# Two layers of attention and routed SwiGLU on one core: gathering early candidates for the eight routed tokens while the last token tile is projected

## The chip, the cores and the metric

The kernel runs on one core of one Trainium2 chip, and the seven other cores are idle. The metric is the device time of one execution in microseconds. The time shown for the kernel before is the median of three runs, 4652.86 us (4651.84 to 4653.18).

The engines named below are PE (TensorE, matrix products, with PEld for its weight loads), DVE (VectorE), ACT (ScalarE), POOL (GpSimd) and SP (SyncE, which only issues transfers). A transfer is issued on the queue of SP, ACT or POOL. Each engine works through its own instructions in the order in which the program lists them.

## The reference

The sequence has 2048 tokens of width 1024, all in float32. Four blocks follow one another, with x carried along: attention, routed feed-forward, attention, routed feed-forward, the same weights both times. "Layer 0" and "layer 1" below are the two pairs.

```python
def A(x, wqkv, wo):                  # 32 heads of 32
    q, k, v = split(x @ wqkv)
    return softmax(q @ k.T * 32 ** -0.5) @ v @ wo        # per head
def B(x, w_r, w_gate, w_up, w_down): # F = 3584
    r = x @ w_r                      # one score per token
    idx = argsort(-r)[:8]            # the eight best of 2048 tokens
    x_sel = x[idx]
    y = (silu(x_sel @ w_gate) * (x_sel @ w_up)) @ w_down
    return x + scatter(y * sigmoid(r[idx]), idx)         # other rows: x
x = A_x
x = x + A(layernorm(x)); x = x + B(layernorm(x))
x = x + A(layernorm(x)); x = x + B(layernorm(x))
```

What is computed for the eight tokens needs all of w_gate, w_up and w_down: 44 MB, read once per layer.

## The kernel before, in words

Each layer has three stages: projection of q, k and v; attention over 32 units of 16 key tiles; and the output projection, a loop over 16 token tiles `t` of 128 rows. The output loop (lines 922 to 960) multiplies a tile by `wo` in three passes, each of 16 matmuls of 512 columns: `woh` with the high part of the attention output, `woh` with the low part, `wol` with the high part. Then DVE adds the residual (L934), takes mean and variance (L130, L132), POOL takes the power -0.5 (L134, L135), DVE normalises into `xn` (L951) and reduces `xn` times `w_r` into one column of `rcols` (L952): the router scores of the tile. POOL writes mean and factor of each row to `mr` (L943 to L946), which goes to the DRAM tensor `mrd` (L949), adds `x + xn` (L953), and the sum is stored to the layer's output (L956). SP issues both stores, except in tile 15 of layer 1, where ACT does.

After the loop `route` runs. `top8` finds the eight best scores: PE transposes `rcols` (L280), DVE takes the best eight of each tile (L283), spreads them over one row by a product with `own` (L284, L286), takes the best eight of that row and their places (L289, L290), and turns places into token numbers by small products (L293 to L312). Two gathers by POOL (L197) then read the eight rows of the output, `bg`, and their mean and factor, `mg`, from DRAM. DVE rebuilds the normalised rows (L347), PE transposes them in eight pieces (L350), and DVE copies the result into `xs` (L351), the stationary operand of the feed-forward.

In layer 0 `exchange` runs between: the eight routed rows change places with the last eight rows of the sequence, so that layer 1 can start on tiles 0 to 14 before the feed-forward of layer 0 is done. It gathers rows into `tg` and scatters them (L197, L201). Layer 1 begins by loading tiles 0 to 2 of its input (`xt`, SP, L74), normalising them (L130 to L563) and transposing them on PE (L572), after five steps of layer 0's feed-forward and four more; the rest of that feed-forward is spread between the matmuls of the q, k, v projection. In layer 1 `back` undoes the exchange with two gathers and two scatters, and the feed-forward follows by itself, up to the end of the kernel.

The feed-forward is a list of steps, each with one weight tile of 1 MB at most: `g` and `u` (gate and up, eight each, for columns 0 to 2047 and then for the rest, rows of 8 KB and 6 KB), `t` (transposes) and `d` (down: for each half of 512 output columns seven tiles of 512 rows by 512 columns, 2 KB a row), `y` (the sum over four row groups by a product with `sel`, L413, the gate factor and the residual, L415). Each step multiplies on PE (L376, L403); down steps add up in SBUF on DVE (L409). Weight tiles are loaded by SP (L184 for down, L188 for gate and up). In layer 1 22 tile slots exist: ten of their own, loaded during the output loop, and twelve that stand on the tiles of the output loop as these come free (`ord` after tile 13; `woh`, `wol`, `ohl` after tile 15). Another load can start only when a step has used up its tile.

Of the kernel before, what the change touches and what calls it, by code (L numbers as in the profile page):

```python
# [19 lines left out]
NT = S // 128  # L20
# [37 lines left out]
def tile_kernel(ctx, tc, x, wqkv, wo, w_r, w_gate, w_up, w_down, out):  # L58
# [42 lines left out]
    sel = cons.tile([128, 8], F32, name="sel")  # L101
    dve.tensor_add(sel, ident[:, 0:8], ident[:, 32:40])
    dve.tensor_add(sel, sel, ident[:, 64:72])
    dve.tensor_add(sel, sel, ident[:, 96:104])

    triu = cons.tile([128, 128], F32, name="triu")
# [5 lines left out]
    ones_c = cons.tile([8, 128], F32, name="ones_c")  # L112
    pool.memset(ones_c, 1.0)
# [4 lines left out]
    pool.iota(first_of, pattern=[[1, 1]], base=0, channel_multiplier=128, allow_small_or_imprecise_dtypes=True)  # L118
    ones16 = cons.tile([NT, 128], F32, name="ones16")
    pool.memset(ones16, 1.0)  # L120
    PERM = {}
# [16 lines left out]
    class FeedForward:  # L138
# [6 lines left out]
        def __init__(self, n, dst, mrd):  # L145
# [7 lines left out]
            for b in range(2):  # L153
                self.steps += [("d", b, c) for c in range(7)] + [("y", b, 0)]
# [20 lines left out]
        def load(self, eng=sync):  # L175
# [7 lines left out]
            if k == "d":  # L183
                eng.dma_start(t.rearrange("p (i m) -> p i m", i=4),  # L184
                              w_down[a * 512:(a + 1) * 512, h * 512:(h + 1) * 512].rearrange("(i p) m -> p i m", p=128))
            else:
                w = (w_gate if k == "g" else w_up)[a * 128:(a + 1) * 128, h * 2048:min((h + 1) * 2048, F)]
                eng.dma_start(t[:, 0:w.shape[1]], w)  # L188

        def more(self, wp, names):  # L190

            self.pools += [(wp, i, k) for i, k in names for _ in range(k)]
            for _ in range(sum(k for _, k in names)):
# [13 lines left out]
        def exchange(self, sb, idx):  # L207
# [6 lines left out]
            dve.tensor_scalar(ne, sb[:, 2:10], tcol, None, op0=OP.not_equal)  # L214
# [5 lines left out]
            pe.matmul(p[0:8, 0:1], triu[0:8, 0:8], ni, start=True, stop=True)  # L220
            pe.matmul(p[0:8, 8:16], ltb, triu[0:8, 0:8], start=True, stop=True)
# [15 lines left out]
            tg = self.tmp.tile([8, D], F32, name="tg")  # L237
# [33 lines left out]
        def top8(self, rcols):  # L271
# [3 lines left out]
            t = self.tmp.tile([128, D], F32, name="x", bufs=3) if n else self.tmp.tile([NT, 512], F32, name="t8")  # L275
            r16, vals, toks = (t[0:NT, 128 * i:128 * i + 128] for i in range(3))
            row = t[0:1, 384:512]
            rows8 = lambda a: a.rearrange("p (a b) -> p a b", b=8)
# [716 lines left out]
```

## Time and profile before

| | |
|---|---|
| median of three runs | 4652.86 us |
| profiled execution | 4661.98 us |
| its span, first to last instruction | 4660.2 us |
| output loop and `route` of layer 0: last product of tile 15 to first matmul of layer 1's projection | 2246.2 to 2280.2 us |
| the same of layer 1: last product of tile 15 to first product of the feed-forward | 4552.7 to 4581.5 us |
| feed-forward of layer 1, to its last scatter | 4581.5 to 4652.9 us |

Times in the profile count from the start of the span. A row of a timeline gives start, duration, engine, line, operation, what it writes and reads, shapes, the number of instructions merged, and in brackets the idle time of the engine before and what ended it. PEq, SPq and so on mark the issuing part of an engine. A row of the windows view gives the length of the stretch, the busy time and instructions of each engine (PE, PEld, DVE, ACT, POOL), then the granted TensorE clock as a share of full speed, the share of the 16 DMA engines that was busy, and the GB/s they moved.

### The profile page before, as it was taken

Reading aid. Unit: us, or ns where it says so; the run is one execution under the profiler, and the core shown is the slowest. Engines: PE = TensorE matmul, PEld = TensorE weight load, DVE = VectorE, ACT = ScalarE, POOL = GpSimd, SP = SyncE. Lnnn points to the kernel's source line nnn. Section 1 sums busy time; section 2 is a strip of 40 time slices with the busy share of each in tenths; the row PEclk is TensorE's granted clock in tenths of the full one; section 3 lists DMA queues with packets and bytes.
Section 4 is the critical chain, followed back from the end, with each engine's and each line's share of the span. In section 5 each row is a group of like instructions: output and inputs, shape, how many; then the busy total and the mean of one; then the engine's idle time right before and its main releaser. Section 6 shows DMA issues by size and latency. Waiting matters only on the chain. (4 is left out here: it accounts for less than half of the span.)

```text
span 4660.2 us, 76410 instructions
## 1 busy us (share of the span) xinstructions
PE 4536.3 (97%) x30704; PEld 2758.9 (59%) x30704; DVE 3169.7 (68%) x4855; ACT 2430.3 (52%) x2564; POOL 3214.3 (69%) x1240
## 2 busy tenths in 40 slices
PE   8999999999999999989899999999999999999995
PEld 8888755555555555548677887555555555554581
DVE  2211588888888888866422215888888888887762
ACT  2222266766767676750122222776766767677400
POOL 4444378988989888944433342898889889898441
PEclk9999999999999999999899999999999999999997
DMA  5766476776867777759689674777777768676698
GB/s 184 207 183 192 137 168 147 172 158 151 180 147 169 161 168 156 176 119 263 196 255 277 199 206 128 163 169 155 169 150 168 164 146 182 149 168 160 149 252 307
DMA packets 350899, 833.40 MB, mean 179 GB/s; under 512 B 43760, under 2 KB 192240, under 8 KB 301376
## 3 DMA queue, kind: packets, MB, share of 16 engines
q1 hardware_dynamic: 297216, 477.44, 35.7%
q0 software_dynamic: 44960, 325.34, 34.3%
q10 hardware_dynamic: 8368, 25.73, 2.1%
q8 instruction: 241, 3.95, 0.4%
q14 instruction: 114, 0.93, 0.1%
HBM read 384.07 MB, written 119.24 MB: 108 GB/s over the span
## 5 line engine op out<-in xcount | busy, mean ns | idle before, releaser
L503 DVE TENSOR_REDUCE nm<-st 128x1 f32<-128x512 f32 x3896 | 2419.0, 683 | 402.2 <-PE st L495 396.1
L819 ACT ACTIVATE P<-pre 128x1024 f32<-128x1024 f32 x2048 | 1986.2, 1022 | 716.1 <-PE pre L510 517.8
L755 POOL TENSOR_TENSOR acc<-acc,P 128x2048 f32<-128x2048 f32 x434 | 2104.0, 4848 | 80.0 <-DMA P<-P 71.8
L510 PE MATMUL pre<-q,ks 64*128 64x512 f32 (+1 forms) x8192 | 1141.6, 396 | 4.2 <-ACT P L819 4.2
L745 PE MATMUL pv<-P,v 128*32 128x512 f32 x8192 | 1091.0, 605 | 2.6 <-DMA v<-vd 2.6
L495 PEld LDWEIGHTS st<-ks,q 64*128 64x128 f32 x3896 | 542.6, 184 | 905.2 <-DVE nm L503 764.7
L495 PE MATMUL st<-ks,q 64*128 64x512 f32 x3896 | 975.8, 470 | 0.5
L549 POOL TENSOR_TENSOR wl<-wraw,wh 128x2048 fp32r<-128x2048 f32 (+1 forms) x101 | 443.3, 4391 | 657.0 <-ACT wh L548 616.7
L510 PEld LDWEIGHTS pre<-q,ks 64*128 64x128 f32 (+1 forms) x8192 | 774.2, 186 | 185.5 <-ACT P L819 57.2
L758 POOL DMA_DIRECT2D P<-P x310 | 297.1, 958 | 261.4 <-PE st L495 192.0
L604 DVE TENSOR_TENSOR lo<-st,hi 128x512 fp32r<-128x512 f32 x128 | 88.3, 690 | 526.6 <-ACT hi L603 517.4
L589 PE MATMUL st<-xh,wh 128*128 128x512 f32 x1024 | 408.3, 399 | 0.0
L589 PE MATMUL st<-xh,wl 128*128 128x512 f32 x1024 | 399.7, 390 | 4.2 <-POOL wl L549 4.2
L589 PE MATMUL st<-xl,wh 128*128 128x512 f32 x1024 | 399.6, 390 | 0.0
L603 ACT CAST hi<-st 128x512 fp32r<-128x512 f32 x128 | 75.3, 588 | 550.4 <-PE st L589 546.2
L745 PEld LDWEIGHTS pv<-P,v 128*32 128x32 f32 x8192 | 161.8, 108 | 259.1 <-issue 253.5
L755 POOL TENSOR_TENSOR acc<-P 128x2048 f32<-128x2048 f32 x62 | 294.6, 4751 | 8.4 <-DVE nm L503 4.5
L589 PE MATMUL st<-wh,xh 128*128 128x256 f32 x1024 | 294.2, 287 | 2.3 <-ACT wh L548 2.0
L589 PE MATMUL st<-wl,xh 128*128 128x256 f32 x1024 | 291.2, 284 | 2.1 <-POOL wl L549 2.1
L589 PE MATMUL st<-wh,xl 128*128 128x256 f32 x1024 | 290.9, 284 | 0.8 <-DVE xl L575 0.8
L929 PE MATMUL pre<-woh,ohl 128*128 128x512 f32 x1024 | 245.3, 397 | 20.0 <-DVE pre L952 13.0
L589 PEld LDWEIGHTS st<-xh,wh 128*128 128x128 f32 x1024 | 192.4, 188 | 74.5 <-issue 27.9
(228 smaller groups left out, 3186.8 us busy)
## 6 DMA issues: line engine op xcount, KB each, us to landing
P<-P POOLq DMA_DIRECT2D x310, 1024.0 KB, 8.9
wraw<-in_A_wqkv_dram SPq DMA_DIRECT2D x96, 1024.0 KB
q<-qh SPq DMA_DIRECT2D x256, 128.0 KB
ks<-kh SPq DMA_DIRECT2D x112, 256.0 KB
vd<-vn SPq DMA_DIRECT2D x64, 256.0 KB
qh<-hi SPq DMA_DIRECT2D x64, 256.0 KB
ql<-lo SPq DMA_DIRECT2D x64, 256.0 KB
kh<-hi SPq DMA_DIRECT2D x64, 256.0 KB
```

Of the source, the lines that this page charges most:

```text
L495: pe.matmul(ps[b], Q[u][rows, i, 0, qt * 128:(qt + 1) * 128], KS[(u // QC) % 2][rows, i, 0, j * 512:(j + 1) * 512], start=True, stop=True, ...
L503: dve.tensor_reduce(NM[u][:, j, 2 * i + b:2 * i + b + 1, qt], ps[b], axis=AX.X, op=OP.max, negate=True)
L510: pe.matmul(p[:, b * 512:(b + 1) * 512], KS[(u // QC) % 2][rows, i, slot, kt * 128:(kt + 1) * 128], Q[u][rows, i, slot, :], start=(slot == ...
L549: pool.tensor_tensor(wl[:, sl, :], raw[:, sl, :], wh[:, sl, :].bitcast(F32), op=OP.subtract)
L589: pe.matmul(p, *pair(a, l, r), start=(a == 0 and k == 0), stop=(a == KD - 1 and k == 2))
L603: act.copy(hi, p)
L604: dve.tensor_tensor(lo, p, hi.bitcast(F32), op=OP.subtract)
L745: pe.matmul(PV[u][32 * h:32 * h + 32, :], V[g][:, kt, 32 * h:32 * h + 32], P[s][:, h, :], start=(kt == 0), stop=(kt == NT - 1), tile_posit ...
L755: (dve if on_dve else pool).tensor_tensor(o, a, P[u * NT + k].rearrange("p h c -> p (h c)"), op=OP.add)
L758: pool.dma_start(P[u * NT + a], P[u * NT + b], accum_op=OP.add)
L819: act.activation(P[s][:, 2 * i:2 * i + 2, :].rearrange("p h c -> p (h c)"), p, AF.Exp, scale=SCALE)
L929: pe.matmul(p[:, bl], l[:, a, :], r[a][:, bl], start=(k == 0 and a == 0), stop=(k == 2 and a == KD - 1))
```

## The change

Five edits go together, in both layers unless said.

1. `top8` is gone. `candidates` finds the best eight of tiles 0 to 14 in three parts while tile 15 is projected: the first part stands in front of the third matmul pair of the third pass, the second in front of the seventh pair, the third between the normalisation and the score reduction of tile 15. It ends with gathers of the eight candidates' output rows and of their mean and factor.
2. `route` takes the best eight of these eight and of the 128 scores of tile 15. The rows of `xs` come by one-hot matrix products: for each of eight pieces of 128 columns one product of `xn` (tile 15, still in SBUF) with a 128 x 8 selection and one of the candidates' rows with an 8 x 8 selection, in place of eight transposes. In layer 1 the token numbers, the gather of `bg`, `back` and `token` come after `xs`; in layer 0 they and `exchange` come before.
3. Down weights come as full rows: 14 tiles of 256 rows by 1024 columns, 4 KB a row, with the two column halves side by side in the row groups of PSUM, so one list of 14 `d` steps and one `y` step with two products by `sel` and two DVE operations.
4. In layer 1 one `ohl` slot is loaded after tile 14, and tile 14's two stores go from SP to ACT. Tile 15 writes no `mr` and no `mrd` row in either layer.
5. Layer 0 closes the loop's tiles after `route`, and `route` has its scratch in them; `sel` has two columns of eight and a few constants are new.

```diff
+        def candidates(self, rcols, wp):
+            tiny, m = self.tiny, NT - 1
+            t = wp.tile([128, D], F32, name="x", bufs=3)
...
+            pe.transpose(p[0:m, 0:128], rcols[:, 0:m], ident)
+            dve.tensor_copy(r, p[0:m, 0:128])
...
+            dve.max(m16, r)
+            dve.tensor_tensor(rows8(vals), own[0:m, 0:m, :], m16[:, None, :].to_broadcast([m, m, 8]), op=OP.mult)
+            yield
+            p = ps_st()
+            pe.matmul(p[0:1, 0:8 * m], ones16[0:m, 0:1], vals, start=True, stop=True)
...
+            dve.max_index(mi, final[:, 0:8], row)
...
+            dve.tensor_tensor(rows8(toks), own[0:m, 0:m, :], f16[:, None, :].to_broadcast([m, m, 8]), op=OP.mult)
+            yield
+            p, c = ps_st(), slice(0, 8 * m)
+            pe.matmul(p[:, 0:8], ones_c[0:1, :], mif, start=True, stop=True)
+            pe.matmul(p[c, 16:24], toks, ones16[0:m, 0:8], start=True, stop=True)
+            pe.matmul(p[c, 24:25], vals, ones16[0:m, 0:1], start=True, stop=True)
...
+            self.rows = wp.tile([128, D], F32, name="x", bufs=3)[0:8]
+            self.mg = tiny([8, 2], "mg")
+            self.gather(self.rows, idx, self.dst[0:S - 128, :])
+            self.gather(self.mg, idx, self.mrd[0:S - 128, :])
...
+            pe.transpose(p[0:1, 0:128], rcols[:, NT - 1:NT], ident)
+            dve.tensor_copy(final[:, 8:136], p[0:1, 0:128])
...
+            if not n:
+                sb, PERM["routed"] = tokens()
+                self.exchange(sb, idx=PERM["routed"])
+            dve.tensor_scalar(self.rows, self.rows, self.mg[:, 0:1], self.mg[:, 1:2], op0=OP.subtract, op1=OP.mult)
...
+                pe.matmul(p[:, a, 0:8], xn[:, sl], pl, start=True, stop=False)
+                pe.matmul(p[:, a, 0:8], self.rows[:, sl], pc, start=False, stop=True)
+            dve.tensor_copy(xs[:, :, 0:8], p[:, :, 0:8])
...
-                eng.dma_start(t.rearrange("p (i m) -> p i m", i=4),
-                              w_down[a * 512:(a + 1) * 512, h * 512:(h + 1) * 512].rearrange("(i p) m -> p i m", p=128))
+                eng.dma_start(t.rearrange("p (i m) -> p i m", i=2),
+                              w_down[a * 256:(a + 1) * 256, :].rearrange("(i p) m -> p i m", p=128))
...
+                part = ffn.candidates(rcols, wp) if t == NT - 1 else None
                 for k, (l, r) in enumerate(((oh, woh), (ol, woh), (oh, wol))):
                     for a in range(KD):
+                        if part and k == 2 and a in (2, 6):
+                            next(part)
...
+                if n and t == NT - 2:
+                    ffn.more(wp, (("ohl", 1, 2),))
...
+                store = act if n and t >= NT - 2 else sync
+                if t < NT - 1:
...
                 dve.tensor_scalar(xn, x2, mv[:, 0:1], rs, op0=OP.subtract, op1=OP.mult)
+                if part:
+                    list(part)
                 dve.scalar_tensor_tensor(p, xn, 1.0, wrb, op0=OP.mult, op1=OP.mult, accum_out=rcols[:, t:t + 1])
```

More of the change, by code (lines that the diff above doesn't have):

```diff
@@ L190, in more @@
         def more(self, wp, names):
[L192 to L193 removed]
+            self.pools += [(wp, i, bufs) for i, k, bufs in names for _ in range(k)]
+            for _ in range(sum(k for _, k, _ in names)):
                 self.load()
```

205 lines of the change are left out of this document (98 added, 107 removed).

## The prediction

> **What bounds the kernel now.** I read the page first: PE is busy for 97% of the span, so between the two routed blocks nothing but PE time counts, and the change touches no matmul there. It touches two places where PE stands still: behind the output loop of layer 0, and from the output loop of layer 1 to the end. So next I read the chain that ended last and, of the stretches that it passes through, the windows view. The third fence is a timeline of the kernel's end.
>
> ```profile
> span 4660.2 us, 76410 instructions
> PE 4536.3 (97%) x30704; PEld 2758.9 (59%) x30704; DVE 3169.7 (68%) x4855; ACT 2430.3 (52%) x2564; POOL 3214.3 (69%) x1240
> ```
>
> ```profile
> 4572.73 6.44 DMA mg<-mrd,idx
> ...
> 4579.27 0.81 DVE x L347
> ...
> 4580.12 1.03 PE st L350 x8
> ...
> 4581.52 8.48 PE pv L376 x64
> ...
> 4591.16 7.12 PE pv L376 x64
> ```
>
> ```profile
> 4546.00:4552.00 6.00, 6.00 (x28) 4.99 (x27) 1.67 (x3) 0.00 (x0) 3.95 (x3) 1.00 1.03 431
> 4552.00:4558.00 6.00, 0.68 (x3) 0.22 (x2) 4.24 (x6) 0.00 (x0) 2.18 (x6) 0.92 1.05 189
> 4562.00:4570.00 8.00, 1.85 (x10) 1.57 (x10) 3.10 (x20) 0.00 (x0) 0.00 (x0) 0.50 1.03 359
> 4582.00:4586.00 4.00, 4.00 (x32) 1.03 (x28) 0.00 (x0) 0.00 (x0) 0.87 (x1) 0.71 0.46 115
> 4586.00:4590.00 4.00, 3.95 (x40) 0.88 (x32) 0.00 (x0) 0.00 (x0) 0.00 (x0) 1.00 0.87 314
> 4590.00:4600.00 10.00, 7.96 (x71) 2.55 (x74) 4.66 (x4) 1.07 (x2) 1.28 (x1) 1.00 1.01 412
> 4606.00:4642.00 36.00, 23.18 (x156) 4.83 (x150) 11.97 (x14) 2.24 (x4) 1.28 (x1) 0.91 1.05 387
> ```
>
> ```profile
> 4632.88 1.06 PE L403 MATMUL st<-wol,ht 128*32 128x512 f32 x8 [1.65 <-DMA wol<-in_B_w_down_dram]
> ...
> 4649.10 1.88 PE L413 MATMUL st<-xn,sel 128*8 128x512 f32 x2 [0.80 <-DVE xn L409]
> ```
>
> The chain names a gather, the rebuilt rows, the transposes and then PE, which suggests that every microsecond cut before 4581.5 is won. The windows say otherwise. From 4546 to 4642 the transfers are full, except in two holes: 4552 to 4558 at 189 GB/s and 4582 to 4590 at 115 and 314. Down steps wait for their weights (1.65 us before a product of 1.06), and the end follows the last weight tile. So in layer 1 I count bytes and holes, and an earlier first product is worth only the hole that it closes. In layer 0 weights do not bind, and there the time to the next matmul counts.
>
> **The change part by part: the tail of tile 15, both layers.** The parts of `candidates` are put between other work of PE and DVE, so their price is their rows from today's `top8`:
>
> ```profile
> 4548.89 3.79 PE L929 MATMUL pre<-wol,ohl 128*128 128x512 f32 x16
> 4557.29 1.23 DVE L952 SCALAR_TENSOR_TENSOR pre<-xn,wrb 128x1024 f32<-128x1024 f32 x1
> 4559.06 0.28 DVE L281 COPY x<-st 16x128 f32<-16x128 f32 x1 [0.47 <-PE st L280]
> ...
> 4559.69 1.31 DVE L284 TENSOR_TENSOR x<-own,m 16x128 f32<-16x128 f32 x1
> ...
> 4561.05 0.58 PE L286 MATMUL st<-x,ones 16*1 16x128 f32 x2 [2.04 <-DVE x L284]
> ...
> 4561.67 0.28 DVE L287 COPY x<-st 1x128 f32<-1x128 f32 x1 [0.67 <-PE st L286]
> ...
> 4563.59 0.28 DVE L297 TENSOR_TENSOR x<-own,f 16x128 f32<-16x128 f32 x1
> 4563.80 0.21 DVE L299 TENSOR_SCALAR pick<-st,pos 128x8 f32<-128x8 f32 x1
> ...
> 4563.93 0.59 PE L301 MATMUL st<-ones,x 16*128 16x8 f32 x2 [0.43 <-DVE x L297]
> 4564.38 0.56 PE L302 MATMUL st<-ones,x 16*128 16x1 f32 x2
> ...
> 4564.97 0.17 DVE L304 COPY cand<-st 128x9 f32<-128x9 f32 x1 [0.96 <-PE st L302]
> ...
> 4565.66 0.14 DVE L332 CAST idx<-sb 8x1 int32<-8x1 f32 x1
> ```
>
> The third pass starts at 4548.89 with 0.24 us a matmul. Part one stands four matmuls in, at 4549.8; its transpose and DVE work (4559.06 to 4561.00, 1.94 us, hidden in DVE's idle time) end at about 4552.2. PE reaches part two at 4552.1, waits 0.15 for it, multiplies for 0.6, and has four matmuls left: the pass ends at 4553.8, 1.1 late. But DVE is then in part two, which takes what lies between 4561.67 and 4563.87, 2.2 us from 4552.9; the residual add starts at 4555.1, 2.4 late. Part three adds 0.21 for the selection and 0.83 from L304 to L332, 1.05 us in front of the score reduction. The reduction ends at 4562.0 for 4558.5: **3.45 us later**, in both layers.
>
> **Layer 1, the first product.** The candidates' index is there 1.3 us before, at 4560.7. POOL's gathers are issued by 4561.1 and 4562.4 (1.04 and 0.3 apart now); the second lands 6.44 later, at 4568.9. The eight remaining picks of `route` on PE and DVE (transpose, maximum, place, broadcast: an estimate of 2.9 us from rows L281 to L299 above) are done at 4564.9, under that landing. Then 0.81 rebuilds the rows, and of the 16 one-hot products 15 remain. Their nearest rows are L301 and L302, also float32 on a 128-column stationary: 0.45 from start to start, at a granted clock of 0.50 in that window. Fifteen take 6.75 at that clock and 3.4 at full; the feed-forward went from 8.48 us for its first 64 records to 7.12 for the next 64, so the clock rises inside. I take 5.2, against 1.03 for the eight transposes now. With 0.4 for the copy the first product starts at 4575.3, 6.2 us before 4581.5.
>
> What that buys: the queue ran dry at 4582 and 4582 to 4586 lost (412-115)x4 us, 1188 KB or **2.9 us**. The slots now come free from 4576 on, while the stream is still running, and I keep 0.3 of hole: -2.6. Bounds: 0 if the start stays, -3.8 if the 0.95 us of 4586 to 4590 go too. I leave these, as the scatters of `back` stand there now and will follow.
>
> **Tile 14's store on ACT's queue.** Both are stores of 512 KB under streaming loads, but on SP's queue the stretch around it lost (431-189)x6, 1452 KB or 3.4 us, and tile 15's on ACT's queue (431-359)x8, 576 KB or 1.3 us. I take the difference, **-2.1**; bounds 0 and -3.4. The Trainium skill, "DMA: Bandwidth & Descriptors", section "Issuing engines are not separate DMA queues", says that transfers run on the same 16 engines whichever engine issued them, and that another issuer saves only the issue time. By it this term would be 0. The two rows differ, but also in what was queued around them, so it keeps a chance below. Its wait moves to ACT, where nothing but the next stores is queued. The four `mr` operations and the row store of tile 15 go, 2 us of POOL beside DVE's work: 0. The earlier `ohl` load moves no bytes: 0, covered by the stream.
>
> **Down weights in 4 KB rows.** 3584x1024x4 bytes are 14.68 MB, at 387 GB/s 37.9 us. A row of 2 KB at 387 takes 5.3 ns of the whole stream, one of 6 KB at 412 14.9, so one of 4 KB some 10.0: 410 GB/s, 35.8 us, **-2.1**. Bounds: 0, and -3.8 at the 431 of 8 KB rows. The Trainium skill, same page, section "Specifications", puts the least transfer for line rate at 512 B. By that this term would be 0 too; the trace disagrees, with 387 for 2 KB rows and 412 and 431 for longer ones.
>
> **The end.** Both column halves are now summed after the last down step. A second product by `sel` follows the one of 1.88; its two passes add 1.7 at the half clock (bounds 0.85 at full clock and 1.88), **+1.7**. Down steps have the same products and one DVE add more, under the loads: 0.
>
> **Layer 0.** Here the restart of PE counts:
>
> ```profile
> 2252.03 2.34 POOL L953 TENSOR_TENSOR x<-x,xn 128x1024 f32<-128x1024 f32 x1
> ...
> 2259.71 1.10 POOL L197 DMA_INDIRECT bg<-x,routed  x1 [4.63 <-DVE ne L214]
> ...
> 2262.80 0.86 POOL L197 DMA_INDIRECT tg<-x,abi  x1 [0.81 <-DVE sg L346]
> 2266.20 0.90 POOL L201 DMA_INDIRECT x<-tg,abi  x1 [2.53 <-DMA tg<-x,abi]
> ```
>
> ```profile
> 2254.39 0.32 SPq L956 DMA_DIRECT2D x<-x  x1
> ...
> 2268.75 1.29 SPq L74 DMA_DIRECT2D xt<-x  x3
> ```
>
> ```profile
> 2267.24 8.45 PE L376 MATMUL pv<-fw,xs 128*32 128x512 f32 x64 [0.39 <-DVE xs L351]
> 2276.96 1.07 PE L376 MATMUL pv<-fw,xs 128*32 128x512 f32 x8 [1.26 <-ACT fy L384]
> 2277.95 1.97 PE L572 MATMUL pre<-ident,xt 128*128 128x128 f32 x16
> ```
>
> Two chains meet at 2277.95. One runs over POOL: the add of tile 15 (2252.03) now stands behind the two candidate gathers, whose index is there at 2254.2; with 2.3 us for both it starts at 2256.9 and ends at 2259.3, and tile 15's store goes out 5 us late, as do the two `wraw` loads behind it on SP. The store had landed within 5.3 us (2254.39 to 2259.71); with 4 it lands at 2263.3, so `bg` and then `tg` start at 2263.4 and 2264.8, 2.0 late; `exchange`, whose second operand waits for POOL's add too, is done by 2263.3, under that landing. `tg` then meets the `wraw` loads, which costs another 1, and the scatter and the `xt` loads come 3 late. Some 1.4 of that is slack before the transposes of the second tile: +1.6. The other chain: the selection, `exchange`, the rows and the 15 products put the first product at about 2270 for 2267.24, and its 8.45 shrink to 7.1, since PE is warmer: +0.5 to +2.2. I take **+2.0**; bounds 0 and +7.2 (below).
>
> Sum: -2.6 -2.1 -2.1 +1.7 +2.0 = -3.1. The profiled execution took 4661.98 us, 1.8 over its span, and would take 4658.9. The median of the runs is 9.1 below it, so 4652.86 becomes **4649.8**.
>
> **The rivals.** (a) Slower: layer 0's `tg` and scatter land as slowly as such transfers do in layer 1 under loads.
>
> ```profile
> tg<-x,abi POOLq DMA_INDIRECT x1, 2.5
> ...
> x<-out_dram,abi POOLq DMA_INDIRECT x1, 6.2
> ...
> out_dram<-wrb,routed POOLq DMA_INDIRECT x1, 5.4
> ```
>
> Then 2264.8+6.2+0.9+5.4 puts the `xt` loads at 2277.3, 8.6 late, 7.2 behind the slack: -5.1+7.2 gives 4655.0. It decides from 5.1 us lost in layer 0 on. For it, the `wraw` loads move exactly there; against it, `tg` took 2.5 beside their end. (b) The hole stays: the candidates' gather waits for tile 14's store, and if that lands after 4567, the first product is back at 4581.5: 4652.4. (c) One of two terms is nothing: tile 14's store costs 3.4 us on either queue, since what made tile 15's cheaper was the traffic around it, or down rows stream at 387 GB/s whatever their length. Either gives 4651.9. This is what the two rules of the Trainium skill named above would make of it. (d) More is won: nothing lost in layer 0, both halves of the hole closed, down rows at 431 and a store that costs nothing, with 0.85 at the end: -3.8-3.4-3.8+0.85, 4642.7.
>
> **How the numbers follow.** Chances: 0.50 for my sum (its own range 4646 to 4653), (a) 0.13, (b) 0.13, (c) 0.14, (d) 0.10. About 0.2%, 9.3 us, is what a measurement of this kernel can tell from no change. Only (d) reaches beyond on the fast side, 0.10 with its neighbours; on the slow side (a) together with (b), or a stall that no row shows, 0.07; 0.83 lies between. The range 4642.5 to 4657 takes in (d) and (a).
>
> **What would show it.** Right: the score reduction of tile 15 3.5 us later in both layers; 15 spaced products on `xs`; the first feed-forward product of layer 1 near 4575 by the old clock; no stretch at 115 GB/s behind it; some 410 GB/s in the down steps; two products by `sel` at the end. Wrong: a hole that stays or moves, down steps at 387, the store of tile 14 still draining the stream, or `xt` loads of layer 0 over 6 us late.

## The result, and the profile after

The changed kernel takes 4667.22 us (median of 22 runs, 4657.02 to 4670.89), the kernel before 4656.49 (22 runs beside them, 4651.30 to 4664.93). The ratio is 1.0016 (1.0011 to 1.0022): slower by 0.16%, some 7.5 us. (The ratios here and below are estimates from all the runs, with their 95% interval, and not quotients of the two medians, which lie 10.7 us apart.) The forecast was 4649.8 with a range up to 4657.0, a gain of 3.1 us, so the time went the other way and out of the range. Part of the distance is the starting point: the forecast counted from 4652.86, the median of three runs, and the median of 22 is 3.6 us above it.

A single execution says little here: the runs of either kernel spread over some 14 us, and the profiled ones stand on opposite sides. Before's (4661.98) lies 5.5 above its median, after's (4658.61) 8.6 below. The comparisons below therefore go by medians and by stage lengths that repeat over many traces.

The page of the changed kernel, its span and engine lines:

```profile
span 4656.8 us, 76547 instructions
PE 4556.0 (98%) x30764; PEld 2767.3 (59%) x30764; DVE 3173.6 (68%) x4875; ACT 2429.2 (52%) x2562; POOL 3218.6 (69%) x1237
```

PE is busy 19.7 us more than before, with 60 instructions more. The 32 one-hot products, 0.52 us each, less the 16 transposes that they replace (1.03 a layer) make 14.7 of it. The other 5 us lie in the two projections, work that the change left alone, and the experiments go after that too.

The timeline of the changed kernel around tile 15 of layer 1 (start, duration, engine, line):

```profile
4546.27 7.42 PE L959 MATMUL pre<-woh,ohl 128*128 128x512 f32 x32
...
4555.37 0.27 DVE L285 TENSOR_TENSOR x<-own,m 15x120 f32<-15x120 f32 x1
...
4564.26 1.21 DVE L987 SCALAR_TENSOR_TENSOR pre<-xn,wrb 128x1024 f32<-128x1024 f32 x1
4565.08 1.32 POOL L199 DMA_INDIRECT x<-out_dram,idxa  x1 [2.44 <-DMA woh<-in_B_w_up_dram]
...
4566.70 0.87 POOL L199 DMA_INDIRECT mg<-mrd,idxa  x1 [0.30 <-issue]
...
4567.03 3.19 DVE L337 CAST mif<-mi 1x8 f32<-1x8 uint32 x1
4567.59 2.36 POOL L988 TENSOR_TENSOR x<-x,xn 128x1024 f32<-128x1024 f32 x1
...
4572.42 0.80 DVE L363 TENSOR_SCALAR x<-x,mg 8x1024 f32<-8x1024 f32 x1 [1.10 <-issue]
4573.27 0.59 PE L368 MATMUL st<-pick,x 8*128 8x8 f32 x2 [1.44 <-DVE x L363]
...
4580.60 0.59 PE L368 MATMUL st<-pick,x 8*128 8x8 f32 x2
...
4581.58 2.79 PE L403 MATMUL pv<-fw,xs 128*32 128x512 f32 x12
...
4645.57 1.88 PE L441 MATMUL st<-xn,sel 128*8 128x512 f32 x4 [0.80 <-DVE xn L437]
```

Counted from tile 15's first product, the rebuilt rows are ready 26.95 us on (4573.22), 11.5 us earlier than before (38.44). But the fifteen one-hot products behind them take 7.8 us at an even 0.52 each, where eight transposes took 1.03. So the first feed-forward product comes 35.3 us after tile 15's first, for 39.9: 4.6 us won. The windows view of the same kernel, for the stretches shown of before (that of the tile-14 store, the hole, what follows it, the down steps):

```profile
4556.00:4562.00 6.00, 2.93 (x15) 1.65 (x13) 4.59 (x14) 0.00 (x0) 0.17 (x1) 0.92 1.01 387
4582.00:4586.00 4.00, 4.00 (x28) 0.95 (x24) 0.87 (x7) 0.00 (x0) 1.77 (x2) 0.64 0.59 173
4586.00:4590.00 4.00, 4.00 (x40) 0.96 (x32) 0.00 (x0) 0.00 (x0) 0.61 (x1) 1.00 0.89 306
4606.00:4640.00 34.00, 23.24 (x157) 4.97 (x151) 11.94 (x14) 1.65 (x3) 1.27 (x1) 0.90 1.03 409
```

Down weights stream at 409 GB/s for 387, the stretch at 189 GB/s is gone, and the hole is shallower in this pair (173 for 115) but still there. Over the traces of all the kernels below, the first two hold and the third does not. In like stretches of each trace, laid by its own tile 15 and its own first feed-forward product, the down steps have 386 or 387 GB/s in all eight traces with rows of 2 KB and 408 to 410 in all ten with rows of 4 KB; the stretch behind tile 14's store has 187 to 219 in the eight without edit 4 and 359 to 412 in the ten with it; but the hole has 98 to 186 in the eight without candidates in layer 1 and 99 to 168 in nine of the ten with them. So the first product of layer 1 came earlier as forecast, and the hole moved with it. In layer 0 PE's restart was late:

```profile
2252.93 3.18 DVE L337 CAST mif<-mi 1x8 f32<-1x8 uint32 x1
2253.50 2.35 POOL L988 TENSOR_TENSOR x<-x,xn 128x1024 f32<-128x1024 f32 x1
...
2260.74 0.82 DVE L363 TENSOR_SCALAR x<-x,mg 8x1024 f32<-8x1024 f32 x1
...
2261.61 0.59 PE L368 MATMUL st<-pick,x 8*128 8x8 f32 x2 [1.39 <-DVE x L363]
...
2268.93 0.59 PE L368 MATMUL st<-pick,x 8*128 8x8 f32 x2
...
2269.84 9.15 PE L403 MATMUL pv<-fw,xs 128*32 128x512 f32 x64 [0.32 <-DVE sg L377]
...
2283.49 0.39 PE L617 MATMUL st<-wh,xh 128*128 128x256 f32 x1 [0.28 <-ACT xh L602]
```

From the last product of tile 15 (2243.9) to layer 1's projection it is 39.6 us, for 34.0 before. A copy of eight numbers that takes 0.16 us elsewhere takes 3.18: it starts beside the issue of the second gather, 0.57 us ahead of POOL's sum of `x2` and `xn`, and ends when the sum has ended. The one-hot products keep 0.52 us from start to start to the end; they do not speed up.

### The profile page after: what moved, and what is told of

It reads as the page before. It is cut to its first block, busy times and chain, and to the rows that moved or that the text cites. A ratio compares the mean times of both kernels' runs of the same rounds, so it can differ in the third digit from the quotient of the medians.

```text
span 4656.8 us, 76547 instructions
## 1 busy us (share of the span) xinstructions
PE 4556.0 (98%) x30764; PEld 2767.3 (59%) x30764; DVE 3173.6 (68%) x4875; ACT 2429.2 (52%) x2562; POOL 3218.6 (69%) x1237
## 4 chain that ended last, share of the span: by engine, by line
PE 88%; DMA 5%; POOL 2%; DVE 2%; issue 2%; ACT 1%; SPq 0%; ACTq 0%; POOLq 0%; DVEq 0%
PE st L617 22%; PE pv L772 21%; PE pre L538 20%; PE st L523 16%; PE st L792 3%; PE pre L959 2%; PE pv L403 1%; DMA ord<-oT 1%; POOL acc L782 1%; DMA ord<-rd 1%; PE pre L523 1%; PE pre L600 1%; DVE ohl L913 0%; DMA x<-x 0%; DMA wraw<-in_A_wqkv_dram 0%
```

## The experiments

### The parts one by one

`e1_down` is the kernel before with the down weights as full rows. It has `triu` as 8x8, as the changed kernel has.

```diff
-    triu = cons.tile([128, 128], F32, name="triu")
+    triu = cons.tile([8, 8], F32, name="triu")
...
-            for b in range(2):
-                self.steps += [("d", b, c) for c in range(7)] + [("y", b, 0)]
+            self.steps += [("d", 0, c) for c in range(14)] + [("y", 0, 0)]
```

> The kernel before with edit 3 alone: down weights in 14 tiles of 256 full rows (4 KB), one list of d steps, two products by sel at the end; to fit, the constant triu is 8 x 8. Theory 1 (the two traces differ by layer 0's restart, 39.6 us against 34.0, and by layer 1's tail, and the timed difference is their sum): down steps of layer 1 stream at 410 GB/s for 387, 2.1 us less for 14.68 MB, and the end costs up to 1.7 more; time 0 to 3 us under the kernel before, layer 0's restart unchanged at 34.0. Rival (full rows cost something in layer 0's copy of the feed-forward, where the steps stand between the projection's matmuls): 3 us or more above the kernel before.

`e2_store` is the kernel before with tile 14's stores on ACT's queue and one `ohl` slot loaded after tile 14.

```diff
+                if n and t == NT - 2:
+                    ffn.more(wp, (("ohl", 1, 2),))
...
-                store = act if n and t == NT - 1 else sync
+                store = act if n and t >= NT - 2 else sync
```

> The kernel before with edit 4 alone: in layer 1 one ohl slot loaded after tile 14 and tile 14's two stores on ACT's queue (tile 15 keeps its mrd row). Theory 1: the stretch behind tile 14's store loses 1.3 us of loads in place of 3.4, time 2 us under the kernel before. Rival (the issuing queue is nothing): no change, and a stretch near 189 GB/s stays.

`e3_cand` is the changed kernel with both of these undone, so the candidates alone.

```diff
-            self.steps += [("d", 0, c) for c in range(14)] + [("y", 0, 0)]
+            for b in range(2):
+                self.steps += [("d", b, c) for c in range(7)] + [("y", b, 0)]
...
-                store = act if n and t >= NT - 2 else sync
+                store = act if n and t == NT - 1 else sync
```

> The changed kernel without edits 3 and 4: candidates and the new route alone, in both layers. Theory 1: layer 0's restart, last product of tile 15 to first matmul of layer 1's projection, is 39.6 us for 34.0 (+5.6); layer 1's first feed-forward product comes 5 us earlier, counted from the start of tile 15, of which the hole in the loads gives 2 to 3 back; time +3 us. Rival 2 (the timed loss of the whole change, 7 to 11 us, lies in this part and in places that the one pair of traces does not show, such as the output loops): +9 us or more.

`e4_after` is the changed kernel itself, with no edit.

> The changed kernel once more, on the chip of the three parts. Theory 1: 7.5 us above the kernel before (ratio 1.0016), and the sum of the three parts within 3 us of it. Its trace again has a restart of layer 0 of 39.6 us and a cast of 3.2 us on DVE in both routes; if the earlier trace was a lucky one, its output loops are longer than 185 and 184 us.

| | median, us | ratio to before (4657.15) |
|---|---|---|
| e1_down | 4648.40 | 0.9979 (0.9970 to 0.9988) |
| e2_store | 4654.89 | 0.9993 (0.9984 to 1.0002) |
| e3_cand | 4656.06 | 0.9997 (0.9988 to 1.0006) |
| e4_after | 4664.20 | 1.0015 (1.0006 to 1.0024) |

The parts add up to 12.1 us less, and the whole is 7.1 us more, by the medians. Nor do the edits' own places explain the parts: with full rows the down steps of layer 1 take 28.4 us from the first product to the last, for 29.8 to 31.9 in the traces of the kernel before and its padded copies, but `e1_down` won 8.8. The rest lies where neither edit is. The projection of layer 0, up to the first product of attention, ends at 591.6 us in `e1_down`, 587.5 in `e3_cand`, 598.0 in `e2_store`, 598.9 before, and 600.6 and 602.9 in the two traces of the changed kernel. From 80 us on PE has hardly a gap there and a granted clock of 0.96 to 1.00, and every trace has the same 1536 products of 512 columns and 1536 of 256.

What differs is the place of the tiles. `triu` shrank from 512 bytes a partition to 32 and the other constants changed too, so every tile that is stacked on the constants lies elsewhere. The projection multiplies the high and the low part of the rows, `xh` and `xl`, by those of the weights, `wh` and `wl`. In layer 0 `wh` and `wl` are stacked from the other end and stay at 163808 and 180192 (bytes in a partition, as the compiled program lists them), while `xh` and `xl` move: `xh` is at 48096 before and in `e2_store`, 47648 in `e1_down`, 47392 in `e3_cand`, 47424 in the changed kernel.

### Only the place

Two kernels with none of the five edits, and two changed kernels, with nothing but padding:

```diff
-    triu = cons.tile([128, 128], F32, name="triu")
+    triu = cons.tile([8, 8], F32, name="triu")
...
+    pad = cons.tile([128, 8], F32, name="pad")
+    pool.memset(pad, 0.0)
```

is `e5_before32`; `e6_before64` has 16 columns for 8. `e7_after96` and `e8_after32` add the two last lines to the changed kernel, with 24 and 8 columns.

> The kernel before with triu allocated as 8x8 and an unused constant of 32 bytes behind the constants: every tile lies at the byte address that it has in e1_down (xh of layer 0 at 47648, 32 bytes past a multiple of 128, instead of 48096, 96 past one; wh and wl stay at 163808 and 180192), and no instruction of the three edits is in it. Theory 1 (the place of layer 0's tiles in SBUF sets the pace of the q/k/v products): the first 600 us end near 590 (587 to 592.5) instead of 598.9, the 256-column products of wh with xl follow each other every 116 ns instead of 122.6, ratio 0.9982 (0.997 to 0.999). Theory 2 (addresses do nothing; e1_down's 591.6 came from its edit or from chance): 598 to 600 us, ratio within 0.0006 of 1. Theory 2 would leave the gain of e1_down to edit 3, of which only 2 to 3.5 us are in the FFN.

> As e5_before32 with 64 bytes of padding: xh of layer 0 at 47680, 64 past a multiple of 128, as in the changed kernel (47424). Theory 1: the first stage ends at 600 to 603 us as in the changed kernel, the 512-column products of xh with wh every 241 ns instead of 233.5, ratio 1.0004 (1.0 to 1.001). Theory 2: 598 to 600 us and 233.5 ns, ratio within 0.0006 of 1.

> The changed kernel with an unused constant of 96 bytes: xh of layer 0 at 47520, 32 past a multiple of 128. Theory 1: the first stage ends at 587 to 592.5 us instead of 600.6 to 602.9, and the kernel takes about 4653 us (4650 to 4656), ratio 0.9993 (0.9985 to 1.0000). Theory 2: 600 to 603 us, ratio 1.0010 to 1.0022 as the changed kernel had.

> The changed kernel with an unused constant of 32 bytes: xh of layer 0 at 47456, 96 past a multiple of 128, as in the kernel before. Theory 1: the first stage ends at 598 to 600 us, 512-column products of xh with wh back at 233.5 ns, ratio 1.0009 (1.0002 to 1.0016), 2 to 4 us under the changed kernel. Theory 2: 600 to 603 us and 241 ns, ratio 1.0010 to 1.0022.

| | median, us | ratio to before (4657.27) | `xh` of layer 0 | first stage, us |
|---|---|---|---|---|
| e5_before32 | 4649.66 | 0.9987 (0.9978 to 0.9997) | 47648 | 590.5 |
| e6_before64 | 4662.47 | 1.0011 (1.0002 to 1.0020) | 47680 | 601.1 |
| e7_after96 | 4664.58 | 1.0020 (1.0011 to 1.0029) | 47520 | 601.8 |
| e8_after32 | 4661.07 | 1.0007 (0.9998 to 1.0016) | 47456 | 604.0 |

`e5` and `e6` differ by 32 bytes of an unused constant and by 12.8 us. That the place does it is shown; the rule by which I chose the paddings is not: `e7`, at 32 past a multiple of 128, should have been quick and was not, and `e8` should have stood at before's 598 to 600 us. Both quick places so far, 47648 and 47392, are 32 past a multiple of 256, and `e7` is not.

Here is how the page of groups shows it: products of layer 0's projection by shape, with busy time and mean ns of one, and the row of attention's products, whose first start ends the stage. The kernel before:

```profile
L589 PE MATMUL st<-xh,wh 128*128 128x512 f32 x512 | 202.8, 396 | 0.0
L589 PE MATMUL st<-wh,xl 128*128 128x256 f32 x512 | 146.0, 285 | 0.0
L745 PE MATMUL pv<-P,v x8192: 592/593/1061, 598.9 to 4360.9; 128*32 128x512 f32 x200
```

The changed kernel:

```profile
L617 PE MATMUL st<-xh,wh 128*128 128x512 f32 x512 | 206.3, 403 | 0.0
L617 PE MATMUL st<-wh,xl 128*128 128x256 f32 x512 | 144.2, 282 | 0.0
L772 PE MATMUL pv<-P,v x8192: 592/593/1061, 600.6 to 4367.9; 128*32 128x512 f32 x200
```

`e5_before32`:

```profile
L591 PE MATMUL st<-xh,wh 128*128 128x512 f32 x512 | 203.4, 397 | 0.0
L591 PE MATMUL st<-wh,xl 128*128 128x256 f32 x512 | 142.2, 278 | 0.0
L747 PE MATMUL pv<-P,v x8192: 592/593/1061, 590.5 to 4351.3; 128*32 128x512 f32 x200
```

No wait is in these rows (the last column is idle time), and a mean differs by 7 ns at most. Products overlap, so the mean is longer than the pace, but the differences carry through: over all six shapes the changed kernel's busy time is 9.3 us above that of `e5`, and its stage ends 10.1 us later.

### The changed kernel at the good place

`e9_after224` pads the constants by 56 columns (224 bytes), which puts `xh` at 47648. `e10_after_pj` leaves the constants and moves the five tiles `xh`, `xl`, `vn`, `hi`, `lo` of layer 0 alone:

```diff
             pw = pst.enter_context(sbuf(f"pj{n}", bufs=2))
+            if not n:
+                pool.memset(pw.tile([128, 56], F32, name="pad", bufs=1), 0.0)
```

`e11_order` is `e9_after224` with

```diff
+                pool.tensor_tensor(x2, x2, xn, op=OP.add)
                 if part:
                     list(part)
                 dve.scalar_tensor_tensor(p, xn, 1.0, wrb, op0=OP.mult, op1=OP.mult, accum_out=rcols[:, t:t + 1])
-                pool.tensor_tensor(x2, x2, xn, op=OP.add)
```

and `e12_layer1` is a combination: the kernel before with edits 3 and 4, and in layer 1 alone the candidates, with POOL's sum in the order of `e11`; 96 unused bytes put `xh` of layer 0 at 47904, 32 past a multiple of 256.

```diff
+                part = ffn.candidates(rcols, wp) if n and t == NT - 1 else None
...
+        ffn.route_last(rcols, xn, wp) if n else ffn.route(rcols, wp)
```

> The changed kernel with an unused constant of 224 bytes, so that layer 0's xh lies at 47648, the very address of e1_down and e5_before32 (32 past a multiple of 256; 47392 of e3_cand, the third one with a short first stage, is 32 past a multiple of 256 too). Theory 1, narrowed by e7_after96 (the place counts to a multiple of 256 bytes and not of 128): first stage 588 to 592.5 us instead of 600.6 to 604, 256-column products every 116 ns, and 9 to 12 us off the changed kernel: ratio 0.9995 (0.9985 to 1.0003). Theory 3 (the three edits themselves spoil the first stage, whatever the address): 600 to 604 us, 120 ns, ratio 1.0010 to 1.0022.

> The changed kernel with the 224 bytes in the pool of layer 0's projection alone: xh, xl, vn, hi and lo of layer 0 lie as in e9_after224, everything else (the constants, the q tiles, attention, layer 1) as in the changed kernel. If these five tiles set the pace: first stage as e9_after224, 588 to 592.5 us, and the same ratio within 0.0008. If another tile moved by the constants does it (q tiles, the small ones): 600 to 604 us and ratio 1.0010 to 1.0022.

> e9_after224 with POOL's sum of x2 and xn put ahead of the two candidate gathers in tile 15 of both layers, so that POOL adds nothing while the last maximum's index is copied. If the 3.2 us of that copy come from POOL's work beside it: the copy takes 0.1 to 0.4 us in both layers, layer 0's restart falls from about 39.5 to 36.5 us (tile 15's last product to layer 1's first), layer 1's first FFN product comes 2 to 3 us earlier after tile 15, and the time falls by 3 to 6 us against e9_after224 (ratio 0.0007 to 0.0013 lower). If the copy is slow for another reason: it stays at 3.2 us and the ratio is that of e9_after224 within 0.0006. The rows of the candidates are gathered up to 2.4 us later for it, which by both is hidden.

> The kernel before with the down weights as full rows, the store of tile 14 on ACT's queue, and the candidates gathered ahead in layer 1 alone (with the order of e11_order); layer 0 routes as before; xh of layer 0 at 47904, 32 past a multiple of 256. By theory 1 and the stages measured so far: first stage 588 to 592.5 us, layer 0's restart 34 to 35.5 us, projection of layer 1 back at 625 to 628.5 us from 631 to 632, layer 1's tail as in e11_order; 4641 us (4637 to 4646), ratio 0.9966 (0.9955 to 0.9978). If the candidates in layer 0 cost nothing, it stands level with e11_order instead, within 0.0008.

| | median, us | ratio to before (4657.04) | first stage, us |
|---|---|---|---|
| e9_after224 | 4655.72 | 0.9997 (0.9988 to 1.0006) | 590.8 |
| e10_after_pj | 4654.74 | 0.9994 (0.9985 to 1.0003) | 591.1 |
| e11_order | 4656.30 | 0.9997 (0.9988 to 1.0006) | 590.4 |
| e12_layer1 | 4646.50 | 0.9975 (0.9965 to 0.9985) | 593.9 |

With 224 unused bytes the changed kernel loses its 7 us, and moving the five tiles of layer 0's projection is enough for it. (Its products read two of the five, `xh` and `xl`; no run moved these by themselves.) The page of `e9_after224`, the same instructions as the changed kernel and one memset more, has PE busy 10.5 us less:

```profile
PE 4545.5 (98%) x30764; PEld 2764.6 (59%) x30764; DVE 3170.8 (68%) x4875; ACT 2429.3 (52%) x2562; POOL 3216.2 (69%) x1238
```

At that place the kernel before has 0.9987 (`e5`), though, so by the middle values the edits still cost 0.1%, some 5 us; but the two intervals overlap. `e12` makes it plainer: without the candidates in layer 0, and at the same distance of `xh` from `wh`, it stands 9 to 10 us below `e9` and `e11`. (It came out 5 us above my 4641: the first stage at 593.9 and not 590, and layer 1's end no better than in `e11`.)

`e11` shortened the copy and won nothing. Layer 0 in its timeline:

```profile
2243.38 2.34 POOL L987 TENSOR_TENSOR x<-x,xn 128x1024 f32<-128x1024 f32 x1 [0.93 <-DVE xn L986]
2244.06 2.74 DVE L990 SCALAR_TENSOR_TENSOR pre<-xn,wrb 128x1024 f32<-128x1024 f32 x1
...
2248.36 0.32 DVE L339 CAST mif<-mi 1x8 f32<-1x8 uint32 x1
...
2254.17 0.80 DVE L365 TENSOR_SCALAR x<-x,mg 8x1024 f32<-8x1024 f32 x1 [0.82 <-DMA x<-x,idxa]
```

The copy takes 0.32 us, beside a gather but no sum, so the sum was what held it. (The other traces agree: the copy of layer 1 takes 3.19 us in four traces, and 0.16 in `e4`, `e8` and `e9`, where it ended before the second gather and the sum had begun.) But the score reduction now runs beside POOL's sum and takes 2.74 us for 1.21. The gathers go out later and their landing ends the chain. In layer 1 that wait is larger, and the first feed-forward product comes 36.9 us after tile 15's first, for 36.1 in `e9`:

```profile
4559.69 1.80 POOL L201 DMA_INDIRECT x<-out_dram,idxa  x1 [0.21 <-issue]
...
4567.57 0.80 DVE L365 TENSOR_SCALAR x<-x,mg 8x1024 f32<-8x1024 f32 x1 [4.02 <-DMA x<-out_dram,idxa]
```

The Trainium skill, "SBUF — State Buffer", section "Who interferes with whom", says that a DVE instruction with two SBUF inputs contends with a POOL instruction that reads SBUF, that a cast can contend too, and that issue order decides who blocks. These rows agree that both kinds are held: 3.18 us for a cast and 1.53 more for the reduction, each beside a sum of 2.35. On the order they show less, since the cast had started before the sum did. Moving the sum moved the wait to another instruction. That the late gathers would be hidden, as my expectation had it, was wrong.

The second cost of the candidates in layer 0 is in the projection of layer 1. From its first product to attention's it takes 630.7 to 631.8 us in all eight traces with the candidates in layer 0, and 625.4 to 628.5 in the six without, at the same distances of the tiles (told below). One step of it shows in the waits of PE, the changed kernel first and then `e5_before32`; over all of them this pause is 2.2 to 2.4 us in the eight and 0.7 to 1.1 in the six:

```profile
PE st L617 <- POOL wl L577: 2.3, 1, 2.3
```

```profile
PE st L591 <- POOL wl L551: 0.8, 1, 0.8
```

One weight block is split later, since its load, issued at the same place, lands some 1.6 us later (by the start of the split). PE then stands for 2.3 us and not 0.8, and starts again at a lower clock, which the windows view of the changed kernel shows:

```profile
2775.00:2780.00 5.00, 4.97 (x15) 3.93 (x16) 0.00 (x0) 1.90 (x1) 2.10 (x1) 0.66 0.64 227
```

By these rows that makes some 3.2 us, 1.5 of pause and 1.7 at the lower clock (an estimate: a third of 5 us). Why this load is later when layer 0 has gathered candidates is not settled. Another 2.4 us went in the first 50 products of the projection, against `e5`; against before it is only 0.6.

### Place or distance

In layer 1 `wh` and `xh` are stacked on the same side and move together, and its pace was the same in all runs so far. So the distance of the two operands might count rather than the place. It is `xh` less `wh`, to a multiple of 256: 0 before, 64 in the quick kernels, 96 in the changed one. `e13_gap64`, `e15_gap32_96` and `e16_gap160_192` are the kernel before with a gap ahead of `xh` in the two layers:

```diff
             pw = pst.enter_context(sbuf(f"pj{n}", bufs=2))
+            gap = (16, 16)[n]
+            if gap:
+                pool.memset(pw.tile([128, gap], F32, name="gap", bufs=1), 0.0)
```

(16 columns are 64 bytes; `e15` has 8 and 24, `e16` 40 and 48.) `e14_best64` is `e12_layer1` with a gap of 64 bytes in layer 1.

> The kernel before with a gap of 64 bytes ahead of xh in the projection's pool of each layer, and nothing else: xh less wh goes from 0 to 64 to a multiple of 256 in both. Theory R (the pace of a product goes by the distance of its two operands' addresses): layer 0's first stage as in e5_before32 (589 to 592.5 us from 598.9) and layer 1's 256-column products from a median of 120 ns to 113, its projection from 628 to 620 (617 to 623); 14 to 17 us in all, ratio 0.9968 (0.9955 to 0.998). Theory P (the pace goes by the place of xh alone: 32 past a multiple of 256 is the good one, and here it lies at 48160, 32 past, in layer 0, and at 85024, 32 past, in layer 1): layer 0 the same; but layer 1, which had xh at 32, 64, 96, 160 and 224 past in the runs so far with a median of 120 ns in all of them, stays at 120 ns and 626 to 629 us: ratio 0.9985 (0.9977 to 0.9995).

> e12_layer1 with the gap of 64 bytes ahead of xh in layer 1's projection; layer 0 has that distance already. Theory R: layer 1's projection 627 to 619 us (616 to 622), 256-column products 120 to 113 ns, 4639 us (4634 to 4643), ratio 0.996 (0.995 to 0.997). Theory P: as e12_layer1, ratio 0.9975 within 0.0008, since layer 1 did not answer to xh's place before.

> The kernel before with a gap of 32 bytes in layer 0 and of 96 in layer 1. Theory R: layer 1 paces as layer 0 did at a distance of 96 in the changed kernel, the 512-column products of xh with wh at a median of 237 ns instead of 227 and the 256-column ones at 118 to 119 instead of 120, its projection 2 to 4 us longer (630 to 633). Layer 0 at a distance of 32 has not been seen: between 588 and 604 us. Theory P: layer 1 stays at 227 and 120 ns.

> The kernel before with a gap of 160 bytes in layer 0 and of 192 in layer 1. Theory R: layer 1 paces as layer 0 did at a distance of 192 in e7_after96, medians of 233 ns (512 columns of xh with wh) and 118 (256 columns). Layer 0 at 160 has not been seen: between 588 and 604 us. Theory P: layer 1 stays at 227 and 120 ns.

`e13_gap64` takes 4646.06 us for 4656.04, ratio 0.9974 (0.9963 to 0.9986), and `e14_best64` 4638.65, ratio 0.9967 (0.9955 to 0.9979). `e15` and `e16` ran once each (4666.91 and 4670.76 us), so that only their stages are used here. The lengths of the stages by distance, over all traces:

| `xh` less `wh` | projection of layer 0, us | projection of layer 1, us |
|---|---|---|
| 0 | 598.9, 598.0 | 625.4 to 628.5 (six traces) |
| 32 | 602.2 | |
| 64 | 587.5 to 593.9 (nine traces) | 621.2, 621.0 |
| 96 | 600.6, 602.9, 601.1 | 631.4 |
| 128 | 604.0 | |
| 160 | 604.5 | |
| 192 | 601.8 | 632.3 |

Layer 1 is given without the traces that gather candidates in layer 0. Products of the projection of layer 1 by shape, before and then in `e13_gap64`:

```profile
L589 PE MATMUL st<-xh,wh 128*128 128x512 f32 x512 | 205.5, 401 | 0.0
L589 PE MATMUL st<-wh,xl 128*128 128x256 f32 x512 | 144.9, 283 | 0.8 <-DVE xl L575 0.8
```

```profile
L589 PE MATMUL st<-xh,wh 128*128 128x512 f32 x512 | 206.0, 402 | 0.0
L589 PE MATMUL st<-wh,xl 128*128 128x256 f32 x512 | 141.6, 277 | 0.8 <-DVE xl L575 0.8
```

Layer 1 answered to 64, 96 and 192 bytes of gap as layer 0 had, though `xh` had lain at the same remainders there before without effect. The distance decides, not the place; that was the open point. Against a distance of 0, the mean of the products of 256 columns falls by 5 to 8 ns at 64 and by 1 to 5 at the others; that of 512 columns rises by up to 5 ns at 64 and by 2 to 7 at the others. The pace, from the start of one product to the start of the next, shows it best: its median is 120 ns for 256 columns and 226 or 227 for 512 at a distance of 0, in both layers and in all the traces that have it; 113 or 114 and 226 to 232 at 64; 117 to 120 and 231 to 238 at the others. So layer 1 kept 120 and 227 with the candidates in layer 0, and the 4 us that it lost there are not of this kind. The whole is a gain at 64 alone. (A distance of 224 was not tried, and that the rule repeats every 256 bytes rests on few places.) The traces have weight loads (PEld) running beside products, so two reads at addresses that get in each other's way are a possible mechanism. It is argued, not shown: no run here looks inside PE. The Trainium skill, "SBUF — State Buffer", section "Who interferes with whom", has "PE and ACT never wait on anyone", which is about other engines; no run here contradicts that, but PE's own pace is not free of where its two operands lie.

## Why the prediction was wrong

**The step that failed** stands in its first paragraph: "nothing but PE time counts, and the change touches no matmul there". The second half is true of the instructions and not of their operands: the smaller `triu`, the dropped `ones_c` and the new constants and small tiles moved `xh` and `xl` by 672 bytes against `wh` and `wl`, from a distance of 0 to one of 96, over 3072 products. That cost 3.1 us in the projection of layer 0 (and 10.6 against the mean of the nine traces at a distance of 64). The first half failed too, in the projection of layer 1: there PE waited 2.2 to 2.4 us for a weight block, for 0.7 to 1.1, and the stage lost 4.2 us that belong to the candidates of layer 0 (`e3` has the loss, `e12` has not). Both stages stood at 0 in the sum. The third miss is a size: layer 0's restart, +4.4 for +2.0. No rival had either of the first two; the nearest is "a stall that no row shows", which shared a chance of 0.07 with (a) and (b) together.

**The sum by its terms**, with mean stage lengths over the traces of each kind (layer 0's restart is counted from the start of tile 15's last product, over the ten traces without and seven with candidates there, `e11` left out):

| | forecast, us | measured, us | from |
|---|---|---|---|
| projection of layer 0 | 0 | +3.1 | 598.4 (two traces) to 601.5 (three at a distance of 96) |
| layer 0, tile 15 to layer 1's projection | +2.0 | +4.4 | 35.7 to 40.1 |
| projection of layer 1 | 0 | +4.2 | 627.0 to 631.2 |
| layer 1, from tile 15 to the end | -5.1 | -4.5 | 117.0 to 112.5 (six traces each) |
| sum | -3.1 | +7.2 | the ratios 1.0015 and 1.0016 make +7.0 and +7.5 |

That the sum meets the ratios so closely is partly luck. The stages between, attention and the output loops, spread by up to 7 us from trace to trace, and in the same six traces of each kind their means differ by -0.5 us in layer 0 and -2.2 in layer 1.

So layer 1 was right as a sum, and by its terms it was right in part by luck. One by one:

- *The score reduction 3.45 us later.* It ends 2.3 us later in layer 1. Mechanism right, size too large.
- *The first product at 4575.3, hole -2.6.* Counted from tile 15 it comes 4.6 us earlier and not 6.2. The candidates' gathers landed as forecast (5.6 us after the issue, for 6.4), but the fifteen products take 0.52 us each, 7.8 in all, where the prediction had 5.2 because "the clock rises inside". It does not: the granted clock beside them is 0.50, and the feed-forward behind them starts as cold as without them: its first 64 records take 8.5 to 9.9 us behind one-hot products and 8.4 to 10.0 behind transposes, over all traces and both layers. And what the earlier product was to buy is not there: the hole is as deep as without candidates (99 to 168 GB/s for 98 to 186). The one exception is `e3_cand`, which has the candidates and not edit 4: 358. So it may be that the two terms overlap, since edit 4 moves the stream ahead and it runs dry earlier too; that is argued from one trace.
- *Tile 14's store, -2.1.* The stretch at 189 GB/s is gone in all ten traces with edit 4. But edit 4 holds two things, and no run separates them: by the rows, (387-189)x6 makes 1188 KB more in the stretch, and the `ohl` load that edit 4 puts ahead, which the prediction had at 0, is 1024 KB by itself. So that the queue did it is not shown. In time, `e2_store` has 0.9993 (0.9984 to 1.0002), so a gain of 2 us can neither be shown nor be ruled out.
- *Down rows at 410 GB/s, -2.1.* 408 to 410 measured, for 386 or 387. Rival (c) falls for the rows; `e1_down` against `e5_before32`, at the same addresses, is 0.9979 to 0.9987, with the right sign and within the intervals of both.
- *The second product by `sel`, +1.7.* It hangs on the clock. In the trace shown both products are in a record of 1.88 us (x4), as one was before (x2), at a granted clock of 1.00 for 0.50: nothing. So it is in four traces with edit 3; in the six others, `e4_after` among them, which is the same kernel, the clock is 0.50 there and the record takes 3.58 us, +1.7 as forecast.
- *Layer 0, +2.0.* +4.4. The transfers did as forecast: the `xt` loads go out 3.4 us later, counted from tile 15's last product, for 3. PE's own chain ended last: its first feed-forward product comes 4.9 us later and not 2.8, and its first 64 records take 9.15 us where the prediction had 7.1. Two things in that chain were off: the one-hot products, 2.6 us longer than forecast as in layer 1, and POOL's sum, which I had put behind the gathers and which then holds DVE's copy for 3.0 us. (Not all of the 3.0 counts: `e11` has no such stall, and the restart is as long.) The row was in the prediction and misread: L284's 1.31 us, taken as the price of that instruction, is the same stall beside POOL's L953; without it the instruction takes 0.27 (L285 after).
- *The rivals.* (a), a slower layer 0, had the right sign and place and the wrong mechanism: it named transfers, and the loss is in DVE, PE and the next projection. (b) had the right sign, a hole that stays, and the wrong mechanism: the gathers landed in time. (d) did not happen.

By what was measured, layer 1's -4.5 is made up of about -2 for the down rows, about -3 for the stretch behind tile 14's store, 0 to +1.7 for the end and nothing for the hole. That is an estimate from the GB/s above, not a measurement of each.

**What beats both kernels.** `e14_best64`, 0.9967 (0.9955 to 0.9979): edits 3 and 4, the candidates in layer 1 alone, and 64 bytes of distance in both layers. `e13_gap64`, which is the kernel before and two gaps of 64 bytes, has most of it, 0.9974 (0.9963 to 0.9986); the two intervals overlap.

## What to carry to other kernels

An edit that changes the size of a constant moves every tile stacked on it, and a stage that the edit does not touch can change its pace by about 1%, as layer 0's projection did here (587.5 to 604.5 us, with 598 to 599 before): before a small gain or loss is explained, compare the mean of untouched product groups between the two pages, and pad the allocation back to the old addresses for a fair comparison. When parts add up to another sum than the whole, look outside the edits' own places. A term that one pair of traces bears out, as the shallower hole and the second `sel` product did here, can be gone in the next trace: look at all of them. And a short instruction with an odd duration beside a long one of a neighbouring engine is a stall, not a price: it goes wherever the neighbour's work is moved.

## What was not expected of the hardware

- In these projections the pace of float32 products of 128 rows depends on the distance of their operands' addresses, to a multiple of 256 bytes: 277 and 278 ns a record at 64 for 256 columns, 283 and 285 at 0; for 512 columns in layer 0 396 at 0, 397 at 64, 403 at 96; with no wait in these rows.
- Fifteen products of 0.52 us without a pause, with PE busy 7.7 of 8 us, did not raise the granted clock: 0.50 beside them, and 8.5 to 9.9 us for the first 64 feed-forward records behind, over all traces, for 8.4 to 10.0 without them.
- A pause of 2.3 us in a full PE was followed by 5 us at 0.66 of the clock; one of 0.8 us was not.
- Down weights in rows of 2 KB streamed at 386 or 387 GB/s in eight traces, and in rows of 4 KB at 408 to 410 in ten.
